# Scores of even and odd heads by turns on the two halves of the array's rows, and four products of ones ahead of each chunk's key transposes

## Chip, cores and metric

The kernel runs on one core of a Trainium2 chip. The metric is the device time of one execution in microseconds (us), lower is better; of several runs the median counts. TensorE (PE) multiplies, VectorE (DVE), ScalarE (ACT) and GpSimd (POOL) work elementwise, SyncE (SP) issues DMA transfers. TensorE's clock has two levels, 1.2 and 2.4 GHz; the profile gives the granted share, 0.50 or 1.00.

## What is computed

A causal retention layer, then two mixture-of-experts layers. 8 sequences of 576 tokens, 8 heads of 64; 4608 tokens of width 512; 8 experts each.

```python
def _attn_ref(q, k, v):
    scores = scale * np.matmul(q, k.transpose(0, 1, 3, 2))
    gamma = 1.0 - 2.0 ** (-5.0 - np.arange(H))
    Dmat = np.where(rel >= 0, gamma[:, None, None] ** rel[None, :, :], 0.0)
    return np.matmul(scores * Dmat[None], v)

def _moe_ref(x, w_gate, w_output_gate, w1, w2):       # per token its best expert e
    h = np.maximum(x[mask] @ w1[e], 0.0)
    out[mask] = gate_w[mask, None] * eom[mask, e, None] * (h @ w2[e])

def reference(**kwargs):
    x = _attn_ref(q, k, v)            # as rows of 512
    return _moe2_ref(x=_moe_ref(x=x, ...), ...)
```

## The kernel before

`attention_and_routing` works through 36 chunks of 128 tokens: each sequence has four whole chunks, and the 64-token ends of two sequences share a tail chunk, so nine chunks belong to a pair of sequences. Numbers are kept as a high and a low float16 part, and a product is made of three passes: high by high, high by low, low by high.

The steps of one chunk, by their names in the plan:

- `k_hi`, `k_lo`, `q_hi`, `q_lo`, `vs`, `v_hi`, `v_lo`: scale and split keys, queries, values (ACT the high parts, DVE the low parts of k and q, POOL `vs` and `v_lo`).
- `pt` (`transposes`, L330): eight 128x128 transposes of the split keys into one PSUM tile of tag "pt", of which there is one buffer; `kT` (ACT) copies it out.
- `S0` and `S1` (`scores`, L348): scores of the even heads (rows 0 to 63 of the array) into PSUM bank pa0 and of the odd heads (rows 64 to 127) into bank pa1; four head pairs by three passes, 12 products of 64 rows by 128 columns each. Each bank has one buffer.
- `am0` (DVE, L418) masks the even scores into a float32 tile "a", `av0` multiplies it with v at full precision (L402, "po<-vs,a"). The odd scores are split by `ah1` (ACT, "au") and `al1` (DVE, "al", L280), masked on POOL and multiplied in `av1`.
- `kv` (L375, L377), `Sn` (DVE, L381), `Sh`, `Sl`: the running state; `qS0`, `qS1` (L402, "po<-Sh,qT"): queries by the state of the chunk before.
- `out` (DVE, L429) scales the sum "po" to the chunk's output "xg"; then `sq`, `rs1`, `rs2`, `xh`, `xl` (DVE, L451), a DMA transpose, and `lg` (L460), the routing logits.

The order is written out by hand: `PLAN` holds for every step five "beats", one for each place of a chunk in its sequence (0 to 3 and the tail). Step n of chunk i stands at i + beat, all steps of all chunks are sorted by that number, and each engine runs its own in that order, one after the other. An engine whose next step waits holds up all that is behind it. Before the chunks, `WARM` = 15 products of ones run on TensorE (L134). Each group of four or five chunks then routes its tokens (`route`, small DVE work) and scatters its rows by DMA (L204). After the last group, `experts` runs both expert layers from a program of its own; the change does not touch it.

Of the kernel before, what the change touches and what calls it, by code (L numbers as in the profile page):

```python
# [13 lines left out]
F32 = mybir.dt.float32  # L14
# [5 lines left out]
B, H, S, HD = 8, 8, 576, 64  # L20
D, F, E = 512, 1024, 8
N = B * S
P = 128
# [11 lines left out]
PLAN = {  # L35
    "k_hi": (-2.028, -2.770, -3.081, -2.909, -2.763),
    "vs": (-1.992, -2.348, -3.188, -1.669, -1.282),
    "k_lo": (-1.751, -2.064, -2.527, -2.579, -2.639),
    "q_hi": (-1.097, -1.702, -1.683, -2.485, -2.161),
    "pt": (-1.401, -1.677, -1.460, -1.290, -1.005),  # L40
    "v_hi": (-0.811, -1.371, -1.336, -0.862, -0.420),
    "q_lo": (-0.551, -1.252, -1.482, -1.253, -0.584),
    "v_lo": (-0.297, -1.046, -0.245, -0.372, 0.196),
    "kT": (-1.159, -0.874, -0.403, -0.701, -0.998),
    "S0": (-0.000, -0.451, -0.122, 0.179, 0.057),
    "am0": (0.222, 0.032, 0.531, 0.449, 0.187),
    "S1": (0.334, 0.281, 0.287, 0.260, 0.137),
    "kv": (0.073, 0.524, 0.372, 0.505, 1.633),
    "Sn": (0.230, 0.575, 0.613, 0.695, 6.213),
    "ah1": (0.596, 0.631, 0.385, 0.518, 0.232),  # L50
# [18 lines left out]
FIRST = -3.462, -0.341, 0.344, 0.159, -0.039  # L69
GATES = -5.2, -1.440, -2.415, 1.091  # L70
WARM = 15
STEPS, STEP, LATE, SLACK = 21, 0.1684, 14, 1
SCATTER = 0.225, 0.428
WEIGHTS = 39.36, 39.38, 39.68, 39.83, 43.38, 44.04, 44.13, 45.14, 52.52, 59.82, 70.32, 70.53, 71.67, 73.74, 109.54, 132.91
# [37 lines left out]
def attention_and_routing(tc, st, I, K):  # L112

    nc = tc.nc
# [3 lines left out]
    ps = psum("ps", 1)  # L118
# [6 lines left out]
    ones, tri = K["ones"], K["tri"]  # L125
# [6 lines left out]
    pw = ps.tile([P, 512], F32, tag="pl", bufs=2, name="pm_warm")  # L132
    for n in range(WARM):
        nc.tensor.matmul(pw, ones, ones.unsqueeze(1).to_broadcast([P, 4, P]), start=True, stop=True)  # L134
# [136 lines left out]
    HALF = (slice(0, 64), slice(64, 128))  # L271
# [14 lines left out]
    class Chunk:  # L286
# [38 lines left out]
            self.on("v_lo").tensor_tensor(self.vh[:, 1], self.vs, self.vh[:, 0], op=ALU.subtract)  # L325

        def transposes(self):
            self.pt = ps.tile([P, 8, P], F16, tag="pt", name=f"pt{self.tag}")
            for i in range(8):
                nc.tensor.transpose(self.pt[:, i, :], self.kh[:, i // 4, 2 * (i % 4):2 * (i % 4) + 2, :], id16)  # L330
# [10 lines left out]
        def q_lo(self):  # L341
            lo(self.qT[:, 1], self.qn, self.qT[:, 0], QS)

        def scores(self, r):
            self.pa[r] = ps.tile([P, 512], F32, tag=f"pa{r}", name=f"pa{self.tag}_{r}")
            for hp in range(4):
                for n, (x, y) in enumerate(PASSES):
                    nc.tensor.matmul(self.pa[r][:, hp * P:(hp + 1) * P], self.kT[HALF[r], 4 * x + hp, :], self.qT[HALF[r], y, hp, :], start=(n == 0), stop=(n == 2))  # L348

        def a_hi(self, r):  # L350
            self.au[r] = three.tile([P, 512], F16, bufs=3, tag="au", name=f"au{self.tag}_{r}")
# [113 lines left out]
    for i, x in enumerate(order):  # L465
# [6 lines left out]
        "vs": Chunk.v_scale, "k_hi": Chunk.k_hi, "k_lo": Chunk.k_lo, "q_hi": Chunk.q_hi, "q_lo": Chunk.q_lo, "v_hi": Chunk.v_hi, "v_lo": Chunk.v_lo,  # L472
        "pt": Chunk.transposes, "kT": Chunk.kT_out, "kv": whole(Chunk.kv), "Sn": whole(Chunk.state),
        "Sh": whole(Chunk.state_hi), "Sl": whole(Chunk.state_lo), "out": Chunk.out, "sq": Chunk.squares,
        "rs1": Chunk.row_scale, "rs2": Chunk.row_scale2, "xh": Chunk.x_hi, "xl": Chunk.x_lo, "lg": Chunk.logits,
    }
    for n, f, r in (("S0", Chunk.scores, 0), ("S1", Chunk.scores, 1), ("am0", Chunk.a_full, 0), ("av0", Chunk.av_full, 0),
                    ("qS0", Chunk.qS, 0), ("qS1", Chunk.qS, 1), ("ah1", Chunk.a_hi, 1), ("al1", Chunk.a_lo, 1), ("av1", Chunk.av, 1)):
        parts[n] = lambda x, f=f, r=r: f(x, r)
    for n, part in (("mh1", 0), ("ml1", 1)):  # L480
# [5 lines left out]
    for i, x in enumerate(order):  # L486
        for L in "kqv":
            add(i - 5.5, x.load, L)
        for n, beats in PLAN.items():
            when = beats[x.c]  # L490
            if i >= NT - 2:
                when = {"qS0": PLAN["S1"][x.c] - 0.001, "qS1": PLAN["av1"][x.c] + 0.001}.get(n, when)
            if n in ("k_hi", "k_lo", "q_hi", "q_lo", "vs", "v_hi", "v_lo") and i < len(FIRST):
                when += FIRST[i]
            add(i + when, parts[n], x)
# [923 lines left out]
def build(nc, I, off, outs):  # L1419
    with ExitStack() as st:  # L1420
        sb = lambda n, s, dt: st.enter_context(nc.sbuf_tensor(n, s, dt))[:]
        K = {"off": off}
        K["cst"] = sb("cst", [P, max(b for _, b in off.values())], F32)
        K["ones"], K["tri"] = sb("ones", [P, P], F16), sb("tri", [P, P], F16)
        K["wg2"] = sb("wg2", [P, 4, 24], BF16)
        K["bias"] = sb("bias", [P, 16], F32)
        K["reg1"] = sb("reg1", [1, 24], I32)
        K["zero"] = sb("zero", [P, XW], F32)
        K["wb0"] = sb("wb0", [P, 2, 8192], F16)
        K["xs1"] = nc.dram_tensor("xs1", [E * R, XW], F32, kind="Internal").ap()  # L1430
        K["xs2"] = nc.dram_tensor("xs2", [E * R, XW2], F32, kind="Internal").ap()
        with tile.TileContext(nc) as tc, ExitStack() as s2:
            attention_and_routing(tc, s2, I, K)
        experts(nc, st, I, K, outs[0])
# [46 lines left out]
```

## Time and profile before

| | us |
|---|---|
| median of 3 runs | 1159.72 (1156.94 to 1166.53) |
| the profiled execution | 1168.55, span 1166.8 |
| PE busy in the span | 1083.7 (93%) |
| DVE busy | 572.4 (49%) |
| ACT busy | 441.6 (38%) |
| POOL busy | 334.0 (29%) |

How the rows below are read. The page's second part cuts the span into 40 slices of 29 us; a digit is tenths. A row of the view by windows has the stretch in us from the span's start, its length, then the busy us of PE, PEld (weight loads), DVE, ACT and POOL with the count of instructions in brackets, the granted clock, the busy share of the DMA engines, and GB/s; where one line is chosen, only the engines that run it stand there. A row of the timeline has the start, the time from the first start to the last end, engine, line, operation, output and inputs, and how many instructions are merged. A row of the waits says who waited on whom: us in total, times, longest. A row of the groups has busy us and mean ns. Matmul durations include the way through the array, so their spacing, not their length, is what one costs in a stream.

### The profile page before, as it was taken

The page shows a single profiled execution, that of the slowest core. Times are in us where ns is not written, and L with a number is a line of the kernel's source. Part 1 is how long each engine was busy: PE and PEld are TensorE (multiplying, and loading weights), DVE is VectorE, ACT ScalarE, POOL GpSimd, SP SyncE. Part 2 cuts the span into 40 slices and gives each one's busy share as a digit, 9 for nine tenths or more (in the row PEclk, how much of TensorE's full clock was granted, in tenths as well). Part 3 has the DMA queues.
Part 4 walks back from the last instruction along what each step waited for, and adds up shares of the span by engine and source line. Part 5 has one row for each costly group of instructions (what it writes and reads, how often), then busy time and mean ns, then how long its engine had stood idle before and what let it go on. Part 6 is the DMA issues. An engine that isn't in the chain of part 4 may idle for free. (4 is left out here: it accounts for less than half of the span.)

```text
span 1166.8 us, 27289 instructions
## 1 busy us (share of the span) xinstructions
PE 1083.7 (93%) x10037; PEld 788.2 (68%) x10037; DVE 572.4 (49%) x1624; ACT 441.6 (38%) x833; POOL 334.0 (29%) x370
## 2 busy tenths in 40 slices
PE   8999889998179999999999989999999999999996
PEld 6888778887156676666666657676766666767664
DVE  6567988996645555555555564641421211111211
ACT  5556656663324343443434433431411111111111
POOL 6456866885511211112121231211001000001000
PEclk6556768685589999999999999999999999999999
DMA  8254756675466665657466646435421121121110
GB/s 286 56 146 91 215 169 166 184 209 154 119 218 184 144 148 143 167 121 188 93 201 156 147 126 156 125 75 170 90 56 55 45 64 38 46 56 54 45 37 30
DMA packets 213056, 145.07 MB, mean 124 GB/s; under 512 B 174089, under 2 KB 174253, under 8 KB 212912
## 3 DMA queue, kind: packets, MB, share of 16 engines
q1 hardware_dynamic: 203952, 114.63, 39.9%
q0 software_dynamic: 8960, 28.62, 6.9%
q8 instruction: 79, 1.29, 0.5%
q14 instruction: 65, 0.53, 0.2%
HBM read 70.75 MB, written 33.92 MB: 90 GB/s over the span
## 5 line engine op out<-in xcount | busy, mean ns | idle before, releaser
L1060 PE MATMUL ph<-xT,wb 128*128 128x256 f16 (+2 forms) x1344 | 339.1, 263 | 22.4 <-PEq L564 22.4
L1061 PE MATMUL ph<-xT,wb 128*128 128x256 f16 (+2 forms) x1344 | 339.2, 263 | 0.0
L1062 PE MATMUL ph<-xT,wb 128*128 128x256 f16 (+2 forms) x1344 | 339.1, 263 | 0.0
L1268 DVE SCALAR_TENSOR_TENSOR hT<-ph,hT 128x512 f16<-128x512 f32 (+2 forms) x168 | 106.5, 638 | 333.7 <-DVEq L564 332.0
L1068 PE MATMUL py<-wb,hT 128*128 128x512 f16 x608 | 230.3, 379 | 1.2 <-issue 1.1
L1070 PE MATMUL py<-wb,hT 128*128 128x512 f16 x608 | 230.4, 379 | 0.0
L1069 PE MATMUL py<-wb,hT 128*128 128x512 f16 x608 | 230.4, 379 | 0.0
L1159 ACT ACTIVATE hT<-ph 128x512 f16<-128x512 f32 (+2 forms) x168 | 92.9, 553 | 227.2 <-ACTq L564 227.1
L1060 PEld LDWEIGHTS ph<-xT,wb 128*128 128x128 f16 x1344 | 131.7, 98 | 40.3 <-issue 23.1
L1061 PEld LDWEIGHTS ph<-xT,wb 128*128 128x128 f16 x1344 | 131.7, 98 | 17.1
L1062 PEld LDWEIGHTS ph<-xT,wb 128*128 128x128 f16 x1344 | 131.8, 98 | 13.1
L1386 POOL DMA_INDIRECT out_dram<-yo,idxo x37 | 35.9, 971 | 333.1 <-POOLq L564 329.7
L1375 POOL TENSOR_SCALAR idx<-v_pos 128x1 int32<-128x1 f32 x39 | 15.4, 394 | 336.3 <-POOLq L564 336.3
L1070 PEld LDWEIGHTS py<-wb,hT 128*128 128x128 f16 x608 | 59.4, 98 | 71.8
L1068 PEld LDWEIGHTS py<-wb,hT 128*128 128x128 f16 x608 | 59.3, 98 | 66.7 <-issue 1.2
L1069 PEld LDWEIGHTS py<-wb,hT 128*128 128x128 f16 x608 | 59.3, 98 | 64.9
L348 PE MATMUL pa<-qT,kT 64*128 64x128 f16 x864 | 84.5, 272 | 7.7 <-DVE al L280 6.1
L1153 ACT ACTIVATE yo<-py,v_gcol 128x512 f32<-128x512 f32 x37 | 25.4, 687 | 168.2 <-ACTq L564 168.2
L576 DVE SCALAR_TENSOR_TENSOR wb<-stg,wb 128x2048 f16<-128x2048 f32 x36 | 82.4, 2290 | 11.0 <-DVEq L564 11.0
L348 PEld LDWEIGHTS <-kT 64*128 64x128 f16 x864 | 69.4, 122 | 13.9 <-DVE al L280 6.8
L1136 ACT ACTIVATE wb<-stg 128x2048 f16<-128x2048 f32 x36 | 68.5, 1901 | 0.0
L1147 ACT ACTIVATE sq<-py 128x512 bf16<-128x512 f32 x39 | 23.3, 597 | 111.6 <-ACTq L564 111.6
(175 smaller groups left out, 1479.9 us busy)
## 6 DMA issues: line engine op xcount, KB each, us to landing
stg<-in_moe_w_dram SPq DMA_DIRECT2D x36, 1024.0 KB, 5.1
kn<-in_k_dram SPq DMA_DIRECT2D x36, 256.0 KB, 6.4
qn<-in_q_dram SPq DMA_DIRECT2D x36, 256.0 KB, 4.5
vn<-in_v_dram SPq DMA_DIRECT2D x36, 256.0 KB, 3.4
w0s<-in_moe_w_dram SPq DMA_DIRECT2D x16, 256.0 KB, 4.7
xs<-zero SPq DMA_DIRECT2D x8, 262.0 KB, 2.7
xs<-zero SPq DMA_DIRECT2D x8, 258.0 KB, 2.9
xT<-xs SPq DMA_TRANSPOSE x42
```

Of the source, the lines that this page charges most:

```text
L348: nc.tensor.matmul(self.pa[r][:, hp * P:(hp + 1) * P], self.kT[HALF[r], 4 * x + hp, :], self.qT[HALF[r], y, hp, :], start=(n == 0), stop=( ...
L576: r = fn(*a, **kw).then_inc(self.sem, 1)
L1060: pe.matmul(o, w1(P_, 0)[:, c, fs], xT[s][:, c, cs], start=(c == 0), stop=False)
L1061: pe.matmul(o, w1(P_, 0)[:, c, fs], xT[s][:, 4 + c, cs], start=False, stop=False)
L1062: m = pe.matmul(o, w1(P_, 1)[:, c, fs], xT[s][:, c, cs], start=False, stop=(c == 3))
L1068: pe.matmul(py[b], hT[:, 0, f, bs], w2(P_, 0)[:, f, :], start=(f == 0), stop=False)
L1069: pe.matmul(py[b], hT[:, 0, f, bs], w2(P_, 1)[:, f, :], start=False, stop=False)
L1070: m = pe.matmul(py[b], hT[:, 1, f, bs], w2(P_, 0)[:, f, :], start=False, stop=(f == 7))
L1136: ac.activation(wb[P_ % 2][:, 0, 2048 * c:2048 * c + 2048], stg[:, 2048 * c:2048 * c + 2048], AF.Copy, scale=WS).then_inc(T["cv_full"])
L1159: ac.activation(hT[:, 0, 2 * g:2 * g + 2, cs], ph[g][:, :, cs], AF.Relu).then_inc(T["hh_full"])
L1268: stt(hT[:, 1, 2 * g:2 * g + 2, cs], ph[g][:, :, cs], 0.0, hT[:, 0, 2 * g:2 * g + 2, cs], op0=ALU.max, op1=ALU.subtract).then_inc(T["h_full"])
L1386: po.indirect_dma_start(out=out, out_offset=bass.IndirectOffsetOnAxis(ap=idxo[b], axis=0), in_=yo[b], in_offset=None, bounds_check=N - 1, ...
```

## The change

The two steps `S0` and `S1` become one step `S`, which takes both PSUM banks first and then issues each product of the even heads followed by the same product of the odd heads. Its beats are near those of `S1`; the beats of `am0` are set behind it. In `transposes`, a tile "fill" with the PSUM tag "pt" is taken first, and `FILL` = 4 products of ones, 128x128 by 512 columns, are written to it; nothing reads it. For the last two chunks `qS0` is placed just ahead of `S`.

```diff
-    "S0": (-0.000, -0.451, -0.122, 0.179, 0.057),
-    "am0": (0.222, 0.032, 0.531, 0.449, 0.187),
-    "S1": (0.334, 0.281, 0.287, 0.260, 0.137),
+    "S": (0.222, 0.181, 0.287, 0.260, 0.097),
+    "am0": (0.334, 0.282, 0.531, 0.449, 0.187),
...
+FILL = 4
...
         def transposes(self):
+            fill = ps.tile([P, 512], F32, tag="pt", name=f"fill{self.tag}")
+            for n in range(FILL):
+                nc.tensor.matmul(fill, ones, ones.unsqueeze(1).to_broadcast([P, 4, P]), start=True, stop=True)
             self.pt = ps.tile([P, 8, P], F16, tag="pt", name=f"pt{self.tag}")
...
-        def scores(self, r):
-            self.pa[r] = ps.tile([P, 512], F32, tag=f"pa{r}", name=f"pa{self.tag}_{r}")
+        def scores(self):
+
+            for r in range(2):
+                self.pa[r] = ps.tile([P, 512], F32, tag=f"pa{r}", name=f"pa{self.tag}_{r}")
             for hp in range(4):
                 for n, (x, y) in enumerate(PASSES):
-                    nc.tensor.matmul(self.pa[r][:, hp * P:(hp + 1) * P], self.kT[HALF[r], 4 * x + hp, :], self.qT[HALF[r], y, hp, :], start=(n == 0), stop=(n == 2))
+                    for r in range(2):
+                        nc.tensor.matmul(self.pa[r][:, hp * P:(hp + 1) * P], self.kT[HALF[r], 4 * x + hp, :], self.qT[HALF[r], y, hp, :], start=(n == 0), stop=(n == 2))
...
-                when = {"qS0": PLAN["S1"][x.c] - 0.001, "qS1": PLAN["av1"][x.c] + 0.001}.get(n, when)
+                when = {"qS0": PLAN["S"][x.c] - 0.001, "qS1": PLAN["av1"][x.c] + 0.001}.get(n, when)
```

## Rows read from the trace of the kernel before

**Rows 1.** The page, part 2, granted TensorE clock in 40 slices.

```profile
PEclk6556768685589999999999999999999999999999
```

**Rows 2.** Windows cut where the granted clock changes; all engines.

```profile
12.00:110.40 98.40, 98.40 (x1144) 86.25 (x1143) 61.07 (x129) 53.77 (x102) 53.72 (x59) 0.50 0.44 135
110.40:130.90 20.50, 17.43 (x352) 15.43 (x352) 20.12 (x44) 15.04 (x31) 17.44 (x18) 1.00 0.81 208
130.90:154.80 23.90, 23.64 (x306) 20.97 (x304) 20.48 (x46) 14.62 (x29) 18.39 (x18) 0.50 0.68 167
154.80:165.00 10.20, 8.39 (x169) 7.38 (x164) 9.56 (x16) 4.75 (x10) 7.32 (x8) 1.00 0.42 157
165.00:185.50 20.50, 18.40 (x214) 16.04 (x214) 14.97 (x45) 13.07 (x26) 12.81 (x14) 0.50 0.66 162
185.50:212.80 27.30, 24.16 (x484) 21.44 (x482) 26.81 (x62) 19.52 (x39) 21.89 (x25) 1.00 0.68 193
212.80:243.50 30.70, 29.90 (x374) 26.56 (x372) 26.69 (x63) 18.63 (x38) 22.57 (x24) 0.50 0.66 181
...
322.30:1166.80 844.50, 809.29 (x6258) 550.28 (x6258) 328.47 (x1021) 259.10 (x478) 128.11 (x155) 0.99 0.43 110
```

**Rows 3.** Windows cut at the starts of L429 of chunks 0, 8, 17, 26, 35.

```profile
28.10:98.00 69.90, 69.90 (x823) 61.76 (x823) 41.34 (x88) 37.99 (x72) 33.73 (x37) 0.50 0.32 85
98.00:166.40 68.40, 61.85 (x974) 54.36 (x972) 61.03 (x137) 42.56 (x84) 50.73 (x51) 0.72 0.65 175
166.40:231.70 65.30, 60.66 (x928) 54.00 (x929) 57.60 (x137) 42.62 (x85) 49.72 (x51) 0.71 0.68 184
231.70:292.60 60.90, 55.75 (x827) 48.51 (x822) 47.49 (x128) 33.29 (x68) 38.13 (x40) 0.67 0.66 175
```

**Rows 4.** Windows of L134 alone, the products of ones: PE, PEld.

```profile
1.14:4.56 3.42, 3.42 (x9) 1.22 (x10) 1.00 0.60 193
4.56:6.30 1.74, 1.69 (x8) 0.60 (x6) 1.00 0.89 222
```

**Rows 5.** Timeline of PE at half clock, from 84 us.

```profile
84.40 0.66 PE L402 MATMUL po<-Sh,qT 64*128 64x64 f16 x9
84.83 0.28 PE L348 MATMUL pa<-qT,kT 64*128 64x128 f16 x1
84.87 0.24 PE L402 MATMUL po<-Sh,qT 64*128 64x64 f16 x1
84.90 0.31 PE L348 MATMUL pa<-qT,kT 64*128 64x128 f16 x1
...
86.21 0.86 PE L375 MATMUL pS<-vh,kh 128*64 128x64 f16 x24
87.00 1.97 PE L402 MATMUL po<-vs,a 128*128 128x64 f32 x8
88.90 1.46 PE L348 MATMUL pa<-qT,kT 64*128 64x128 f16 x12
```

**Rows 6.** Waits of PE, from 124 to 133 us and from 160 to 168 us.

```profile
PE pa L348 <- DVE al L280: 3.1, 1, 3.1
PE po L402 <- DVE eb L439: 3.9, 1, 3.9
```

**Rows 7.** Timeline of PE at full clock, from 248 us.

```profile
249.35 0.84 PE L348 MATMUL pa<-qT,kT 64*128 64x128 f16 x12
...
250.63 1.10 PE L402 MATMUL po<-vs,a 128*128 128x64 f32 x8
...
252.99 0.23 PE L348 MATMUL pa<-qT,kT 64*128 64x128 f16 x1
```

**Rows 8.** DVE: a group by line from 12 to 292.6 us, and timeline rows.

```profile
L282 DVE SCALAR_TENSOR_TENSOR kh<-kn,kh 128x512 f16<-128x512 f32 x34 | 32.4, 954 | 0.0
...
124.20 2.08 DVE L282 SCALAR_TENSOR_TENSOR kh<-kn,kh 128x512 f16<-128x512 f32 x1
...
126.20 1.75 DVE L223 TENSOR_TENSOR dl<-lg,mx 128x40 f32<-128x40 f32 x1
```

More of the change, by code (lines that the diff above doesn't have):

```diff
@@ L474, in attention_and_routing @@
         "Sh": whole(Chunk.state_hi), "Sl": whole(Chunk.state_lo), "out": Chunk.out, "sq": Chunk.squares,
-        "rs1": Chunk.row_scale, "rs2": Chunk.row_scale2, "xh": Chunk.x_hi, "xl": Chunk.x_lo, "lg": Chunk.logits,
+        "S": Chunk.scores, "rs1": Chunk.row_scale, "rs2": Chunk.row_scale2, "xh": Chunk.x_hi, "xl": Chunk.x_lo, "lg": Chunk.logits,
     }
-    for n, f, r in (("S0", Chunk.scores, 0), ("S1", Chunk.scores, 1), ("am0", Chunk.a_full, 0), ("av0", Chunk.av_full, 0),
+    for n, f, r in (("am0", Chunk.a_full, 0), ("av0", Chunk.av_full, 0),
                     ("qS0", Chunk.qS, 0), ("qS1", Chunk.qS, 1), ("ah1", Chunk.a_hi, 1), ("al1", Chunk.a_lo, 1), ("av1", Chunk.av, 1)):
```

## The prediction

> **What bounds the kernel now.** I read the page's clock line first. TensorE runs at the lower of its two levels (1.2 GHz, written 0.50) or between the levels in the slices of the first quarter of the span, and near the full level (2.4 GHz) from then on [rows 1]. The first quarter is the attention and routing stage, the only one that the diff touches; the expert stage takes the last 844.5 us and I carry it over unchanged [rows 2]. Next I cut the attention stage where the granted clock changes [rows 2]. Two kinds of stretch alternate. At half clock, 12 to 110.4 us, PE is busy all 98.4 us while DVE is busy 61.07 (62%) and ACT 53.77 (55%): TensorE sets the pace. At full clock, for instance 185.5 to 212.8 us, DVE is busy 26.81 of 27.3 us (98%) and PE has holes: VectorE sets the pace. So the stage has two limits and the clock chooses between them.
>
> Then I cut it by finished chunks, at the starts of the output products of chunks 0, 8, 17, 26 and 35 [rows 3]. The first eight, all at half clock, take 69.9 us, 8.74 us each, with PE never idle. The next three stretches of nine hold both levels (mean clock 0.72, 0.71, 0.67) and take 68.4, 65.3 and 60.9 us, with DVE busy 61.03, 57.60 and 47.49. Over the 264.5 us of the four, DVE is busy 207.5.
>
> Last, why the clock changes. Before the first rise the engine ran nothing but the fifteen full products of ones: nine in 3.42 us, 0.38 each, then eight in 1.69 us, 0.21 each, those at the edge counted in both [rows 4]. (The clock's record begins only with the rise, so the 1.00 beside the first row is no reading; the halved time is.) The attention has few such products: most use 64 rows or 64 columns [rows 5]. What lowers the clock again is PE waiting: 3.1 us for the DVE product "al" before the fall at 130.9 us, and 3.9 us for DVE before the fall at 165.0 us [rows 6].
>
> **The change part by part.**
>
> *Scores by turns.* Now the twelve products of even heads and the twelve of odd heads stand as two steps. At half clock one step takes 1.46 us including the tail of its last product (about 0.31 us, by the single product of that line), so products start (1.46 - 0.31) / 11 = 0.105 us apart [rows 5]. At full clock it is 0.84 us; with a tail of 0.22 that makes 0.056 us [rows 7]. Do two row halves really work at once? The trace shows it by accident: at 84.83 us, score products on one half of the rows start while state products on the other (nine from 84.40 on, 0.66 us long, and three more) still run, and the two lines alternate [rows 5]. And "kv", which already alternates the two column halves, gets 24 products of 64 columns into 0.86 us [rows 5], where one after the other at half of 0.105 they would take 1.26. So I take the pair at the price of one product: 12 x 0.105 = 1.27 us saved per chunk at half clock, 12 x 0.056 = 0.67 at full. Lower bound nothing (no overlap); upper bound this plus one change of array half, some 0.1 us, which I leave out.
>
> The merged step stands where the odd heads' step stood, at most 0.11 of a chunk earlier, so the even heads' scores come later by up to 0.6 of a chunk in the order. Its first products now wait for both banks: the one that DVE's "a" reads and the one that ACT's "au" and DVE's "al" read. Queued behind it on PE are kv, the full-precision products and the next transposes, and DVE's state product waits for those. Today that wait has hit the odd step alone, 3.1 us at its longest [rows 6]; where it strikes, twelve pairs and not twelve singles are late, so 0.67 us more at full clock, a handful of times: 0 to 3 us over the stage. I take 1.
>
> *Four products of ones.* Each is 512 columns, four times the 128 of a score product: 4 x 0.105 = 0.42 us at half clock, 4 x 0.056 = 0.22 at full. (The fifteen at the start gave 0.38 and 0.21 [rows 4].) Four per chunk: 1.69 us at half, 0.90 at full. They use the transposes' own PSUM slot, so they wait for what the transposes waited for already, ACT's read of the previous chunk's kT; the wait for the split keys (DVE's "kh") comes after them, so where PE stood idle for "kh" they cost nothing. No DMA and no other engine's queue changes.
>
> *Both, at half clock:* +1.69 - 1.27 = +0.42 us per chunk. If the clock stayed as it is, the change would lose. *Both, at full clock:* the ratio of the same steps at the two levels is 0.84/1.46 = 0.58 for scores and 1.10/1.97 = 0.56 for the full-precision products [rows 5, 7]; 8.74 x 0.57 = 5.0 us of PE per chunk, - 0.67 + 0.90 = 5.2. DVE needs 207.5 / 35 = 5.9 per chunk [rows 3]. So at full clock TensorE is no longer last, with the filler in it too; what hides the 0.90 is DVE, and without that cover it would be 36 x 0.9 = 32 us.
>
> *What the filler does to the clock.* It is the largest unknown: no row shows such a filler between attention steps. Rows that bear on it: long runs of full products reach the full clock within their own length [rows 4], and even the present mix reaches it three times in these rows [rows 2]. The filler puts such products into every chunk. I expect the clock to rise within the first chunks and, after each fall, within about one chunk instead of some 24 us (130.9 to 154.8) or 31 us (212.8 to 243.5).
>
> **The sum.** (a) 12 to 28.1 us, PE-bound at half clock: at the ratio 0.57 up to 7 us, but loads and first latencies lie there too; I take -3 (0 to -7). (b) First eight chunks, 69.9 us: PE would need 8.2 x 5.2 = 43, DVE 41.3, ACT 38.0 [rows 3]. Three engines near the same load with waits between them do not reach 98%; I take 85%, 51 us, so -18 (-12 if they take 58 us, -25 at 45). (c) and (d) The middle stretches are DVE's: 61.03 and 57.60 at the 98% of a full-clock stretch are 62.3 and 58.8, -6 each at best; but DVE's own products stretch when POOL is also busy: a key split of 0.95 us in the mean takes 2.08, and 128x40 elements take 1.75 [rows 8]. I take -4 each (0 to -6). (e) The last stretch drains, 47.49 busy: -4 (0 to -12). (f) Merged wait +1, and +2 for chunks that still fall to half clock. Sum: -3 - 18 - 8 - 4 + 3 = -30 us. The wind-down from 292.6 to 322.3 us and the experts move forward whole.
>
> The profiled execution took 1168.55 us (span 1166.8, the rest around it), 8.8 above the median of the three runs, 1159.72. From 1168.6 the sum gives 1138.6; beside the median 1159.7 - 30 = **1130**. The bounds: all best -56, so 1104; all least -12 + 1, so 1148.
>
> **Rivals.**
> *R1, the clock swings.* Each PE wait on DVE drops it, and one chunk's filler isn't enough to raise it. For it: VectorE is the limit at full clock, so waits like the two of [rows 6] come more often, not less. Against it: a fall costs little while PE has slack. If half of the stage stays at half clock, half of the gain stays: 1145, between 1138 and 1153. The Trainium skill ("TensorE: Matmul & The Clock Gate", HAM oscillation) says that a kernel whose matmul bursts are parted by idle gaps is throttled anew in each; the falls behind the two waits agree, and by that rule alone the filler, which queues behind the same waits, would not prevent a fall.
> *R2, the halves don't run at once* in this form (two PSUM banks, both fresh). PE at full clock needs 5.2 + 0.67 = 5.9 per chunk, equal to DVE: some 10 us of the gain go, 1140. Against it: the alternating lines at 84.83 us.
> *R3, slower: the filler pays and the clock doesn't rise.* The place is the front of the transposes, the price 0.42 us per chunk at half clock. Some 23 of 36 chunks run there now: +10; all 36: +15. So 1170 to 1175. It decides if more than about four fifths of today's half-clock chunks stay there: a chunk that changes over saves some 8.74 - 6.6 = 2.1, one that stays loses 0.42, 2.1 / 2.5 = 0.83. For it: PE is busy 100% of 98.4 us already and the clock does not rise.
> A rule that bears on the size: the Trainium skill ("TensorEngine Tiling (Array Packing)", PSUM Bottleneck) warns that packing speeds TensorE up and not the reading of PSUM. The 98% of DVE at full clock agrees; by it the scores' 0.67 us is worth nothing at full clock, and the gain is the clock's alone.
>
> **Chances.** Forecast (clock mostly full, DVE sets the pace) 0.67, 1104 to 1148. R1 0.15, R2 0.05, R3 0.13. This kernel's three runs spread by 0.8%, so about 1%, 1148 and 1171, is what can be told from no change. Faster by over 1%: 0.65 of the forecast, 0.06 of R1, all of R2: 0.76, I say 0.75. Slower: the upper part of R3 and mishaps, 0.09. The rest, 0.16, within 1%. The range 1105 to 1160 holds the forecast, R1 and R2 and leaves out R3 and the best corner.
>
> **What would show it.** Clock: 0.9 or more over 28 to 260 us; if 0.5 to 0.75, R1; if 0.5 in the first hundred, R3. Scores: 24 products in about 1.6 us at half clock or 0.9 at full; over 1.4 at full clock, R2. DVE: over 90% busy in the middle stretches. First eight chunks in 45 to 58 us. Experts: start some 30 us earlier, same length. I would be wrong if the merged step waits on DVE in every chunk, or if DVE's products stretch by as much as they are pulled together.

## The result, and the profile after

The changed kernel takes 1130.82 us (median of 4 runs, 1126.62 to 1134.26); the kernel before 1162.81 beside it (4 runs, 1156.94 to 1166.53). The ratio is 0.9728, 95% interval 0.9667 to 0.9788: 2.7% faster, 32 us. The kernel before spreads by itself, over all runs below from 1145.82 us (granted clock 0.918 over the whole run) to 1177.55 (0.885), and a run over 1.5% above the fastest of its kernel beside it is left out of the ratios, which are therefore not quotients of the medians. The forecast was 1130. The number was right; the experiments below show that half of the reason was not.

First the clock line of the changed kernel's page.

```profile
PEclk9989899875799999999999999999999999999998
```

Then its windows, in the columns of [rows 2]: the stage cut at the same places as [rows 3] (starts of the output products of chunks 0, 8, 17, 26, 35), the whole of that stage, four stretches by the clock, and from the first expert work to the end.

```profile
21.74:70.94 49.20, 43.45 (x878) 34.30 (x873) 46.25 (x90) 37.38 (x73) 41.80 (x42) 1.00 0.52 148
70.94:135.76 64.82, 54.22 (x976) 42.58 (x976) 62.38 (x139) 42.55 (x84) 49.95 (x51) 0.88 0.67 185
135.76:198.47 62.71, 52.26 (x976) 40.78 (x976) 60.56 (x138) 42.44 (x84) 50.14 (x51) 0.93 0.74 192
198.47:255.42 56.95, 50.66 (x829) 41.41 (x829) 49.55 (x127) 32.62 (x67) 36.65 (x40) 0.77 0.76 181
...
21.70:255.40 233.70, 200.61 (x3660) 159.05 (x3655) 218.77 (x486) 155.03 (x308) 178.59 (x184) 0.89 0.68 178
...
12.00:62.00 50.00, 47.83 (x970) 37.85 (x967) 46.95 (x85) 40.73 (x78) 45.36 (x44) 1.00 0.68 210
72.60:79.50 6.90, 6.84 (x84) 5.72 (x83) 4.79 (x16) 4.26 (x9) 5.85 (x6) 0.51 0.98 260
...
130.70:140.90 10.20, 6.62 (x75) 4.71 (x72) 9.81 (x24) 5.09 (x10) 6.48 (x8) 0.50 0.43 116
...
198.90:209.20 10.30, 9.94 (x100) 7.29 (x100) 7.36 (x24) 6.21 (x14) 6.04 (x7) 0.50 0.71 204
...
284.50:1130.90 846.40, 811.04 (x6258) 550.78 (x6258) 328.45 (x1021) 259.31 (x478) 133.25 (x155) 0.99 0.43 110
```

The 98 us at half clock at the start [rows 2] are gone: 12 to 62 us run at the full level. The first eight chunks take 49.2 us where they took 69.9, the three stretches of nine 64.8, 62.7 and 57.0 where they took 68.4, 65.3 and 60.9 [rows 3]. VectorE is now busy 218.8 of 233.7 us (94%), TensorE 86%. What is left at half clock comes in short stretches. In two of those shown TensorE is the limit again (72.6 to 79.5 us, PE 6.84 of 6.9; 198.9 to 209.2 us, 9.94 of 10.3), in the third it is VectorE (130.7 to 140.9 us, DVE 9.81 of 10.2, PE 6.62). The experts are as long as before (846.4 us over this stretch, 844.5 in the like one of [rows 2]).

The same stage of the kernel before, for comparison with the experiments, is one row of its windows:

```profile
28.10:292.60 264.50, 248.16 (x3537) 218.63 (x3537) 207.46 (x486) 156.45 (x307) 172.30 (x179) 0.65 0.57 153
```

Next, timeline rows of the changed kernel's TensorE, at full and at half clock, which answer to [rows 5, 7].

```profile
104.65 0.84 PE L354 MATMUL pa<-qT,kT 64*128 64x128 f16 x24
107.61 1.03 PE L330 MATMUL fill<-ones 128*128 128x512 f16 x4
205.22 1.46 PE L354 MATMUL pa<-qT,kT 64*128 64x128 f16 x24
207.81 1.70 PE L330 MATMUL fill<-ones 128*128 128x512 f16 x4
```

Its TensorE's waits from 6 to 255 us (us in total, times, longest), as in [rows 6]:

```profile
PE pa L354 <- DVE al L280: 13.8, 12, 2.9
PE po L408 <- DVE eb L445: 10.3, 3, 4.4
PE po L408 <- DVE xg L435: 6.4, 4, 2.1
```

And its DVE groups by line (busy us, mean ns), which answer to [rows 8]:

```profile
L457 DVE SCALAR_TENSOR_TENSOR xr<-xg,sc,xr 128x512 f16<-128x512 f32 x33 | 36.3, 1100 | 0.0
L282 DVE SCALAR_TENSOR_TENSOR qT<-qn,qT 128x512 f16<-128x512 f32 x34 | 34.3, 1010 | 0.0
L282 DVE SCALAR_TENSOR_TENSOR kh<-kn,kh 128x512 f16<-128x512 f32 x34 | 33.7, 992 | 0.0
```

In the two steps shown twenty-four score products take the 0.84 us at full and the 1.46 us at half clock that twelve took [rows 5, 7]: the halves do work at once, to the hundredth. The filler is 1.70 and 1.03 us with its tail. TensorE waits for VectorE in earnest: "al" held the merged score step twelve times, 13.8 us, where in the kernel before it held a score step twice, 6.1 us (14 to 292.6 us).

### The profile page after: what moved, and what is told of

Same layout as the page of the kernel before. It is cut to its first block, busy times and chain, and to the rows that moved or that the text cites. A ratio compares the mean times of both kernels' runs of the same rounds, so it can differ in the third digit from the quotient of the medians.

```text
span 1130.9 us, 27578 instructions
## 1 busy us (share of the span) xinstructions
PE 1032.6 (91%) x10181; PEld 723.0 (64%) x10181; DVE 583.4 (52%) x1624; ACT 439.7 (39%) x833; POOL 342.7 (30%) x370
## 5 line engine op out<-in xcount | busy, mean ns | idle before, releaser
L1392 POOL DMA_INDIRECT out_dram<-yo,idxo x37 | 35.9, 970 | 335.1 <-POOLq L570 331.8
L1381 POOL TENSOR_SCALAR idx<-v_pos 128x1 int32<-128x1 f32 x39 | 18.7, 481 | 330.5 <-POOLq L570 330.5
L1385 POOL DMA_INDIRECT xs<-x2row,idx x39 | 49.7, 1274 | 37.5 <-POOLq L570 37.5
L204 POOL DMA_INDIRECT xs<-xr,pi x36 | 45.5, 1264 | 20.3 <-DVE xr L268 7.0
```

Source lines behind the costliest of these rows:

```text
L204: nc.gpsimd.indirect_dma_start(out=rows[x.row], out_offset=bass.IndirectOffsetOnAxis(ap=gr.pi[:, t:t + 1], axis=0), in_=gr.xrow[:, t, :], ...
L1385: po.indirect_dma_start(out=xs2, out_offset=bass.IndirectOffsetOnAxis(ap=idx[b], axis=0), in_=x, in_offset=None, bounds_check=E * R - 1, o ...
```

## The experiments

Theory A is the one on record: the full clock makes the gain, the filler brings the clock, and at full clock VectorE hides both the filler and what the scores save. Theory B: the shorter scores make it and the filler is ballast. Each fence of rows gives a run's attention stage from the start of its first output product to the start of its last, in the columns of [rows 3].

**Each half of the change alone.** The kernel before plus the filler, with `FILL` = 4:

```diff
         def transposes(self):
+            fill = ps.tile([P, 512], F32, tag="pt", name=f"fill{self.tag}")
+            for n in range(FILL):
+                nc.tensor.matmul(fill, ones, ones.unsqueeze(1).to_broadcast([P, 4, P]), start=True, stop=True)
```

> The kernel before with only the four products of ones put ahead of each chunk's transposes; the scores stay two steps. Theory A (the gain is the clock's, and the filler brings the clock): granted clock over the attention stage 0.85 or more, and 1131 to 1142 us, since at full clock VectorE hides the 0.67 us of scores that are not saved. Theory B (the gain is the shorter scores, the filler is ballast): the clock stays at half for most of the stage and the filler costs 1.69 us per chunk there, so 1185 to 1205 us.

The changed kernel without it:

```diff
         def transposes(self):
-            fill = ps.tile([P, 512], F32, tag="pt", name=f"fill{self.tag}")
-            for n in range(FILL):
-                nc.tensor.matmul(fill, ones, ones.unsqueeze(1).to_broadcast([P, 4, P]), start=True, stop=True)
```

> The changed kernel without the filler. Theory A: the clock stays mixed as in the kernel before (0.5 to 0.75 over the stage); the chunks at half clock get 1.27 us shorter and are still TensorE's (7.5 us against 6.2 of VectorE), so 23 x 1.27 = 29 us at the most, 1135 to 1150 us. Theory B: all of the gain, 1126 to 1133 us. If the clock rises without any filler, to 0.85 or more, the filler isn't what raises it.

Filler alone: 1145.9 us, ratio 0.9904 (0.9859 to 0.9949). Turns alone: 1128.23 us, ratio 0.9779 (0.9684 to 0.9873). Their stages, the filler alone first:

```profile
23.60:268.50 244.90, 227.63 (x3662) 181.14 (x3660) 210.98 (x485) 155.48 (x307) 173.91 (x181) 0.89 0.64 166
```

```profile
21.50:248.90 227.40, 186.93 (x3523) 164.44 (x3522) 214.69 (x487) 154.49 (x308) 179.37 (x184) 0.79 0.71 184
```

The turns-only kernel's longest wait of TensorE in its stage:

```profile
PE pa L351 <- DVE al L280: 18.0, 10, 3.7
```

Neither theory came out whole. The filler does raise the clock, 0.65 to 0.89, but at that clock TensorE is still busy 227.6 of 244.9 us (93%) and VectorE 86%: TensorE stays the limit, and 1145.9 lies beyond theory A's 1131 to 1142. The turns in their new place, with no filler at all, raise the clock as well, to 0.79, which theory A had not foreseen (0.5 to 0.75), and they bring the whole gain: VectorE is busy 94% of a stage of 227.4 us. Theory B was right that the whole gain comes without the filler and wrong that the filler must lose: alone it gains 1%. (The 0.65 is from the profiled execution of the kernel before, which at 1168.55 us and 0.893 over the whole run lies above its median, so a rise from the median is somewhat less.)

The two kernels side by side on one chip, five rounds each, unchanged from before:

> The changed kernel as it is, beside the next run on the same chip. Theory C (scores by turns make the gain, the filler gives back in clock what it costs in time): 1128 to 1134 us.

> The changed kernel without the filler, beside the changed kernel on the same chip. Theory C: the same time within 4 us, 1125 to 1133. If the filler were worth its place: slower than the changed kernel by 5 us or more.

1131.0 us (1126.74 to 1137.57) and 1130.28 us (1128.47 to 1134.84); both ratios are 0.9713, intervals 0.9647 to 0.9779 and 0.9651 to 0.9775; the granted clock of the stage was 0.87 with the filler and 0.80 without. Once the scores go by turns, the filler makes no difference that shows.

**What the filler costs and what it gives.** Its cost without its work on the array: the same number of products and columns, on 32 rows and columns.

```diff
-                nc.tensor.matmul(fill, ones, ones.unsqueeze(1).to_broadcast([P, 4, P]), start=True, stop=True)
+                nc.tensor.matmul(fill[0:32], ones[0:32, 0:32], ones[0:32].unsqueeze(1).to_broadcast([32, 4, P]), start=True, stop=True)
```

> The changed kernel with the same number of filler products and columns, but each on 32 rows and 32 columns of the array alone: the same time on TensorE, a sixteenth of the array. Theory A in its strict form (the array's work raises the clock, not TensorE's being busy): clock mixed (0.5 to 0.75), and the filler is paid where the clock is half, so 1150 to 1175 us. If being busy is enough: clock 0.85 or more and the changed kernel's 1131 us.

And twice as much of it:

```diff
-FILL = 4
+FILL = 8
```

> The changed kernel with eight products of ones per chunk, not four: 0.9 us more TensorE work per chunk at full clock. Theory A (VectorE sets the pace at full clock and hides the filler): TensorE comes to 6.1 us per chunk beside VectorE's 6.2, so 1128 to 1145 us. If TensorE were still the limit: 36 x 0.9 = 32 us more, about 1163 us.

The corner filler: 1145.92 us, ratio 0.9936 (0.9886 to 0.9985). Eight products: 1141.8 us, ratio 0.9874 (0.9785 to 0.9962). Stages, corner filler first:

```profile
27.20:274.50 247.30, 221.76 (x3674) 175.30 (x3672) 216.46 (x485) 155.63 (x307) 171.57 (x179) 0.80 0.61 161
```

```profile
24.50:264.50 240.00, 216.83 (x3805) 162.27 (x3806) 219.68 (x486) 155.74 (x307) 174.82 (x183) 0.96 0.63 170
```

A corner product takes as long as a full one (371 to 629 ns each, against 376 to 635). TensorE kept busy in one corner of the array leaves the clock where the turns alone have it (0.80 against 0.79) and costs 18 us (1145.9 against 1128.2). The same columns on the whole array come with a clock of 0.89 and cost 2.6 by the medians, nothing in the run side by side. So in these runs TensorE's being occupied did not raise the clock, and the filler on the whole array did; the full filler gets some 15 of the 18 us back. Both numbers of the corner run lie just outside what theory A's strict form had (0.5 to 0.75, 1150 to 1175 us) and far from what being busy would have given (0.85 or more, 1131). Eight products bring 0.96 and cost 11 us against four, within what theory A allowed, so about two thirds of the further 32 are hidden behind VectorE or got back by the clock. By median, none, four and eight products stand at 1128 to 1130, 1131 and 1142 us.

**Turns, or only the new place?** The merged step stands where the odd heads' stood, takes both banks and saves a change of step. The same without the turns and without the filler:

```diff
-            for hp in range(4):
-                for n, (x, y) in enumerate(PASSES):
-                    for r in range(2):
+            for r in range(2):
+                for hp in range(4):
+                    for n, (x, y) in enumerate(PASSES):
                         ...
```

(The product itself, left out here, is unchanged.)

> Scores in one step at the changed kernel's place, without the filler, but all twelve products of even heads first and then all twelve of odd heads. Theory C (two row halves at work at once): the gain goes, 1150 to 1165 us, with about 2.7 us for the 24 products at half clock. Theory D (the place in the order and the step's taking both banks make the gain): 1126 to 1133 us as with the turns.

1141.32 us (1139.22 to 1161.46), ratio 0.985 (0.9758 to 0.9942): between the two theories. Its stage, and then three of its score steps in the timeline, one at full and two at half clock:

```profile
25.30:260.50 235.20, 212.39 (x3550) 190.47 (x3551) 216.71 (x486) 154.23 (x307) 175.84 (x181) 0.75 0.65 174
```

```profile
49.06 2.29 PE L351 MATMUL pa<-qT,kT 64*128 64x128 f16 x24
...
60.26 1.31 PE L351 MATMUL pa<-qT,kT 64*128 64x128 f16 x24
...
74.14 2.42 PE L351 MATMUL pa<-qT,kT 64*128 64x128 f16 x24
```

By the ratios the step's place gives 1.5% and place and turns together 2.2% on the same chip (0.985 and 0.9779); the intervals overlap, so the split is rough. The profile is clearer than the times: with the place alone TensorE is busy 212.4 us in the stage and the clock is 0.75, with the turns 186.9 and 0.79. Twenty-four products in a row took 2.29 us at half clock in twelve of thirteen unbroken steps and 2.42 in the other, where two separate steps take 2 x 1.46 = 2.92 [rows 5], so being neighbours is worth some 0.6 us a chunk; in the kernel before, too, two score steps stand together so, six times.

What the place gives without a higher clock can be read from the single runs. The kernel before has six runs on that chip with a clock of 0.912 to 0.919 over the whole run; they took 1145.8 to 1149.7 us. Three of the four runs of the place alone have 0.912 to 0.917 and took 1139.2 to 1141.4, some 7 us less at a like clock; the fourth, 1161.46 us, has 0.888. So the place alone does not leave the clocks that the kernel before has by itself. The turns-only kernel does, at 0.923 to 0.933 in all its ten runs.

**Is VectorE the limit?** Theory C, formed on the first four runs: with the scores by turns VectorE sets the pace of the whole stage. On the turns-only kernel, VectorE computes each output product twice:

```diff
             nc.vector.tensor_tensor(self.xg..., self.po, col("gx" + self.sfx)..., op=ALU.mult)
+            twice = two.tile([P, 8, HD], F16, bufs=1, tag="twice", name=f"twice{self.tag}")
+            nc.vector.tensor_tensor(twice, self.po, col("gx" + self.sfx)..., op=ALU.mult)
```

> Scores by turns without the filler, and VectorE computes each chunk's output product a second time into a tile that nothing reads: 0.68 us more on VectorE per chunk, 24 us in all. Theory C (with the scores by turns VectorE sets the pace of the whole stage): nearly all of it shows, 1146 to 1155 us beside 1128. If TensorE or the waits between engines set the pace: at most a quarter shows, under 1135 us.

ScalarE instead copies each output:

```diff
             nc.scalar.activation(sq, self.xg, AF.Square, accum_out=self.of("ss"))
+            twice = two.tile([P, 512], F16, bufs=1, tag="twice", name=f"twice{self.tag}")
+            nc.scalar.activation(twice, self.xg, AF.Copy)
```

> Scores by turns without the filler, and ScalarE copies each chunk's output once more into a tile that nothing reads: 0.6 us more on ScalarE per chunk, 22 us in all. Theory C: ScalarE was busy 68% of the stage and has room, so 1126 to 1135 us. If every engine's latency counts alike, as much as the same work on VectorE costs: 1145 us or more.

And VectorE has less; this kernel leaves out the low part of the queries, and ScalarE writes zeros in its place:

```diff
-            lo(self.qT[:, 1], self.qn, self.qT[:, 0], QS)
+            hi(self.qT[:, 1], self.qn, 0.0)
```

> Scores by turns without the filler, and the low part of the queries is left out: ScalarE writes zeros in its place, so VectorE has 0.8 to 1.0 us less per chunk, about 34 us, and ScalarE 0.6 us more. Theory C: the stage shortens until TensorE (187 us busy of 227) or POOL (179) is the limit, 1100 to 1115 us. If VectorE isn't the limit: 1125 us or more.

More VectorE: 1150.57 us, ratio 0.9942 (0.9904 to 0.998), so 22 of the 24 us show. More ScalarE: 1132.06 us, ratio 0.976 (0.9687 to 0.9834), 4 of 22. Both as theory C had it. One rival is open: the second product also holds the PSUM bank of "po" longer, and TensorE waited for it nine times, 8.0 us, so not all of the 22 us need be VectorE's time alone. Less VectorE: 1123.2 us, ratio 0.9701 (0.9629 to 0.9772), a gain of 5 of the 34 us expected, and that is a miss. Its stage; then from the view of one line, L454 ("xl", the low part of the output), the count and the min/median/max duration in ns; then the group of the key split by line; then that group and the one left out, in the turns-only kernel:

```profile
20.40:235.50 215.10, 177.05 (x3541) 156.51 (x3536) 191.87 (x455) 169.41 (x340) 173.04 (x184) 0.84 0.76 197
```

```profile
L454 DVE SCALAR_TENSOR_TENSOR xr<-xg,sc,xr x36: 733/1090/4962, 33.2 to 239.3; 128x512 f16<-128x512 f32 x36
```

```profile
L282 DVE SCALAR_TENSOR_TENSOR kh<-kn,kh 128x512 f16<-128x512 f32 x32 | 39.1, 1223 | 0.0
```

```profile
L282 DVE SCALAR_TENSOR_TENSOR kh<-kn,kh 128x512 f16<-128x512 f32 x32 | 35.7, 1115 | 0.0
L282 DVE SCALAR_TENSOR_TENSOR qT<-qn,qT 128x512 f16<-128x512 f32 x33 | 28.0, 850 | 0.0
```

The products left out were 28 us in the turns-only stage, not 34, and VectorE's busy time fell by 23: those that stayed grew (the key split from 1115 to 1223 ns), and one of L454 took 4962 ns where the shortest takes 733. In the stage 12 us came off, with VectorE now busy 89% of it; ScalarE, which got the zeros to write, went from 154.5 to 169.4 us, so this run does not show less VectorE work alone. The experts of that execution were 5 us longer, which I did not follow up.

**Two tries at a faster version.** On the turns-only kernel, the row factor "iv" once per group, and then, on top of it, the state's scaling on ScalarE:

```diff
+        v.tensor_scalar(iv[:, g].bitcast(I32), gr.eb[:, g], 8388608.0, 59.0 * 8388608.0, op0=ALU.mult, op1=ALU.add)
         v.tensor_tensor(lg[:, g], lg[:, g], bc(iv, 16), op=ALU.mult)
...
-            v.tensor_scalar(self.of("iv").bitcast(I32), self.of("eb"), 8388608.0, 59.0 * 8388608.0, op0=ALU.mult, op1=ALU.add)
```

> Scores by turns without the filler, and the row factor 'iv' computed once for a group of chunks and not for each: 27 VectorE instructions of 0.14 us fewer, 3.8 us. VectorE as the only limit: 3 to 4 us faster than the turns alone, 1122 to 1129. If the waits between engines share the limit, as the run with less VectorE work suggests (34 us less work, 5 us less time): 0 to 1 us, not to be told from the turns alone.

```diff
-            nc.vector.tensor_tensor(self.Sn, self.pS[:, 0:256].rearrange("p (a d) -> p a d", a=4), gC, op=ALU.mult)
+            for a in range(4):
+                nc.scalar.activation(self.Sn[:, a], self.pS[:, HD * a:HD * a + HD], AF.Identity, scale=col("gC")[:, a:a + 1])
```

> As the run before, and the state's scaling moves from VectorE (0.42 us per chunk, 13 us in all) to ScalarE (four instructions of some 0.25 us per chunk, 32 us). VectorE as the only limit: 10 to 16 us faster than the turns alone, 1112 to 1120. Shared limit: 0 to 4 us faster, or slower if ScalarE's longer step makes the state late.

1134.42 us, ratio 0.975 (0.9687 to 0.9813), and 1137.48 us, ratio 0.9774 (0.971 to 0.9837): neither is faster than the turns alone (0.9713; 4 and 7 us slower by the medians, with overlapping intervals). The stages, in that order:

```profile
21.50:252.90 231.40, 194.07 (x3538) 171.07 (x3535) 215.98 (x459) 154.94 (x308) 179.68 (x184) 0.75 0.68 181
```

```profile
23.80:253.50 229.70, 190.91 (x3550) 168.46 (x3547) 210.94 (x429) 176.06 (x427) 174.89 (x182) 0.77 0.70 179
```

With 28 VectorE instructions fewer in the stage (459 against 487) VectorE was busy 216.0 us, not less than 214.7; with 58 fewer 210.9, but there ScalarE's four instructions of 0.32 us each stand where VectorE's one took 0.41, and the state comes later. So adding VectorE work costs nearly its price, and taking some away gave back a part of it at most: VectorE's busy time isn't work alone. No version here that computes the same beats the changed kernel clear of the noise; without the filler it is as fast and does less.

## Why the prediction was right, and where it was not

*Scores by turns (the price of a pair).* Right: 24 products in 1.46 and 0.84 us, as 12 before. (The sum has 12 x 0.105 = 1.27, which is 1.26.)

*The filler's price.* Right: 4 x 0.42 was forecast at half clock, 1.70 us with the tail measured; at full 0.90 forecast, 1.03 with a tail.

*What the filler does to the clock.* Right in direction (0.65 to 0.89 with the filler alone; the sign was 0.9 or more), and the fear of R3 didn't come true. Wrong in what hung on it. "If the clock stayed as it is, the change would lose" took the present clock as given for shorter scores; they raise it to 0.79 by themselves.

*"The gain is the clock's alone", the scores' 0.67 us "worth nothing at full clock".* The first half of this step failed. The sum gives the gain to the clock that the filler brings; without the filler the scores by turns take 1130.28 us, beside 1131.0 with it. That a sum made so came to the right number is luck in this part.

The second half nearly held as long as the clock was full. The filler alone and the changed kernel can be compared stretch by stretch, the filler alone first, with a stretch at full clock (three chunks) last in each:

```profile
23.60:74.20 50.60, 49.16 (x884) 39.45 (x883) 43.28 (x88) 36.99 (x72) 38.31 (x39) 1.00 0.51 132
74.20:143.90 69.70, 63.69 (x976) 50.85 (x976) 61.99 (x139) 42.52 (x85) 49.39 (x51) 0.85 0.63 172
143.90:212.10 68.20, 62.06 (x976) 48.87 (x976) 59.18 (x137) 42.75 (x85) 49.64 (x51) 0.87 0.69 176
...
187.00:212.10 25.10, 21.82 (x394) 17.86 (x395) 25.04 (x52) 16.39 (x33) 19.18 (x19) 1.00 0.77 181
```

```profile
173.60:198.50 24.90, 18.80 (x391) 14.98 (x391) 24.87 (x55) 16.08 (x33) 20.71 (x21) 1.00 0.64 183
```

In that last stretch TensorE has 3.0 us more to do in the filler-only kernel and the time is 25.1 against 24.9 us, since VectorE is busy all of it. The first eight chunks, all at full clock in both, take 50.6 against 49.2 us; TensorE needs 6.1 us a chunk there, near the 5.9 of R2, and is last by a little. The next two stretches, where the clock falls in both kernels (0.85 and 0.87 against 0.88 and 0.93), take 69.7 and 68.2 against 64.8 and 62.7: nearly all of the 11 us between the two stages (244.9 and 233.7; 236.8 in the changed kernel's second profile). So TensorE's price at full clock was about right; what was wrong is the weight of the falls, which the sum has as 2 us and which make the scores' saving count. That the saving is made at half clock is read from where the time lies, not tried by itself, and the filler-only kernel lacks the new place of the step as well as the turns.

The Trainium skill's warning ("TensorEngine Tiling (Array Packing)", PSUM Bottleneck) agrees with the changed kernel in that VectorE became the limit, busy 94%; but only some 86 of VectorE's 218.8 us there are products that read PSUM.

*The sum, term by term* (forecast, measured in the profiled execution): (a) start up to the first output -3, 21.7 - 28.1 = -6.4; (b) first eight chunks -18, 49.2 - 69.9 = -20.7; (c) -4, -3.6; (d) -4, -2.6; (e) -4, -3.9; (f) +3 as an allowance, which the rows do not part from the others. Together -37.2, of which the wind-down and the experts give back 1.3: the span fell by 1166.8 - 1130.9 = 35.9 against 30, the runs' medians by 32. The profiled execution before lay 5.7 us above its median and the one after 1.8 above, which is the difference between 36 and 32. In (b), 69.9 - 51 is 18.9, where the prediction takes 18.

*The merged wait.* Forecast 0 to 3 us over the stage, "a handful of times"; the wait for "al" came twelve times, 13.8 us. That it cost little because VectorE, for which TensorE waited, was the limit anyway is argued, not tried.

*VectorE's products stretch.* Right: the query split went from 780 to 1010 ns. Over the stage VectorE's busy time rose from 207.5 to 218.8 us for the same instructions, which works against the gain.

*R1* (swings): the clock still falls, but briefly; it was 0.88, 0.93 and 0.77 in the last three stretches. Waits stand ahead of the falls, for instance 4.4 us for VectorE's "eb" before the one at 198.9 us, which agrees with the Trainium skill ("TensorE: Matmul & The Clock Gate", HAM oscillation). What the prediction drew from that rule, that the filler would prevent no fall, is not borne out: the stage's clock was 0.79 without filler, 0.89 with four products and 0.96 with eight. *R2* is refuted by the 0.84 us.

## What to carry to other kernels

When an engine is busy 100% at a low clock, first make its stream denser: products that use half the array, put by turns on both halves, cost the time of one here and came with a higher granted clock with nothing added. Filler that only raises the clock has to pay for itself in the stretches that are still that engine's; measure it beside the dense version and not beside the old one, where it looked worth 1%. A busy share of 94%, with a run in which more work costs, does not prove that less work gains: try both directions.

## What the runs showed of the hardware

The view of single lines of the turns-only kernel (count, min/median/max ns) shows VectorE products of one shape and very different length:

```profile
L282 DVE SCALAR_TENSOR_TENSOR kh<-kn,kh x36: 675/910/3651, 4.7 to 220.5; 128x512 f16<-128x512 f32 x36
L454 DVE SCALAR_TENSOR_TENSOR xr<-xg,sc,xr x36: 734/1061/2116, 35.6 to 252.7; 128x512 f16<-128x512 f32 x36
```

Split by whether POOL was busy for over half of the instruction, L282 (keys and queries) takes 1025 ns in the mean of 58 with POOL busy and 683 in 14 without; L454 takes 1166 (29) and 740 (7). VectorE products that read PSUM don't change: "al" (L280) takes 676 and 674 ns, the output product 680 and 679. The kernel before shows the same (945 against 682 for L282, 1145 against 743 for its L451). So in this kernel VectorE's products between SBUF tiles run some 40 to 60% longer beside POOL, and the two meet more often in the turns-only kernel (58 of the 72 of L282) than in the one before (48). That would explain why VectorE work taken away came back as longer products; that it is the cause was not tried by itself.

Two row halves need not be alternated instruction by instruction to overlap: with twelve and twelve in a row the 24 products took 2.29 us at half clock in most steps, 0.4 less than 24 spacings and a tail would be (24 x 0.105 + 0.2 = 2.7), so the second half began before the first was done.
